# Attention followed by a two-layer block: P^T times V as plain float32 products, one head in each half of the array's columns

## Chip, cores and metric

The kernel runs on one core of a Trainium2 chip. The metric is device time in microseconds (us) for one execution, median over runs. The five engines that matter are TensorE (PE for its matmuls, PEld for its weight loads), VectorE (DVE), ScalarE (ACT), GpSimd (POOL) and SyncE (SP), whose queue issues the DMAs. Each engine works through its own queue in order; semaphores join them.

## Reference

Causal attention over 4 batches of 12 heads, 448 positions, head size 64, then a block with a leaky rectifier over 1792 tokens (768 to 2048 to 768), all in float32:

```
scores = scale * q @ k^T;  scores[above the diagonal] = -1e9
p = exp(scores - max(scores));  p = p / (sum(p) + 1e-9)
x = concat_heads(p @ v)                      # 1792 x 768
h = x @ w_in;  g = max(h, 0) + alpha * min(h, 0)
out = g @ w_out
```

The weights arrive as eight-byte floats and are decoded on the core.

## The kernel before, in words

**Attention.** Heads are worked on in 24 pairs (head 0 and head 1 of a pair, `j` in the code). A row of 448 positions is cut into 4 blocks of `CP` = 112. For a pair the steps are: `LQ`, `LK`, `LV` (loads, SP's queue); `S0` to `S2` (scores, L219: float32 matmuls with 64 rows, head 0 in the upper 64 rows of the array, head 1 in the lower 64); `MXij` (mask, and minimum of the negated scores, DVE, L232); `EXij` (exponential and row sum, ACT, L244); `RC` (reciprocal of the sums, two small DVE instructions, L252 and L253); `NOij` (scaling of a row block, POOL, L195); `PTi` (transposes of row block i through TensorE, L271); copies of the transposed blocks from PSUM into SBUF; `AV0` and `AV1` (the products with V, L313, one per head, both into one PSUM bank, transposed: 128 rows are the 2 x 64 columns of the two heads); `XH` (ACT, L191) and `XL` (DVE, L327), which split the result into a high part in float32r and a rest in float32r, as the matmuls of the second half want them. i is the row block, j the head.

**Products with V before.** For key blocks 0 and 1 (`c` < `NSP` = 2) P^T and V are each split in two float32r parts, and three float32r products are made: high by high, low by high, high by low. The split of P^T is `HIi` (ACT) and `LOi` (DVE, L288, PSUM minus the high part); that of V is `VH` (POOL, L195) and `VL` (POOL, L208). For key blocks 2 and 3 P^T is copied as it is (`FCi`, ACT) and the product is float32, which TensorE runs as two instructions for each matmul. V lies in SBUF with zeros beside it, so that each head's weights are 128 columns wide, of which 64 are zeros: both heads' products then add into the same 128 rows. `open_v` writes those zeros once at the start (three DVE fills, two DVE copies).

**Order.** `ORDER` is a list of steps written out by hand. In iteration n of the loop each entry is issued for pair n minus its lag (the number behind the plus); the letter behind the lag names the engine where there is a choice (a ACT, d DVE, p POOL). Four pairs are in flight: `S` has lag 1, most `MX` and `EX` lag 2, `PT` lag 3, `AV` lag 4. Every engine's queue follows this order. `ED` puts one instruction of the early decoding of the first weights (DVE, POOL or ACT) into each iteration from pair 4. PSUM has 8 banks, all from one pool; an iteration takes 13 of them, so that a product waits until another pair's result was read out.

**After attention.** Hooks (`after(...)`) place the first matmuls of the second half (`h_unit`, L381), their read-outs (`h_out`) and the decoding of further weights among the steps of the last two pairs. Then `h` (L381) and `o` (L415) matmuls alternate to the end.

Of the kernel before, what the change touches and what calls it, by code (L numbers as in the profile page):

```python
# [10 lines left out]
F32 = mybir.dt.float32  # L11
F32R = mybir.dt.float32r
# [4 lines left out]
ALU = mybir.AluOpType  # L17
# [4 lines left out]
CP = 112  # L22
# [2 lines left out]
FIRST = 3  # L25
LOADAT = 4, 12
ORDER = """
NO11+3p AV0+4 LK+1 MX11+2 EX10+2 EX20+2 AV1+4 MX00+2 EX11+2 EX00+2 PT0+3 PT1+3 LV+2 MX21+2 PT2+3 EX21+2 MX31+2 NO31+3p MX30+2 MX01+2 EX31+2 EX01+2 XH+4a NO30+3p PT3+3 HI0+3a XL+4 HI1+3a HI2+3a VL+3p LO0+3 LO1+3 S0+1 S1+1 ED+1 EX30+2 LO2+3 VH+2p FC2+3a LQ+0 RC+2 MX10+1 NO10+2p S2+1 NO21+2p NO01+2p HI3+3a LO3+3 NO00+2p NO20+2p MX20+1 FC3+3a
"""


# [1 line left out]
def kernel(  # L33
# [14 lines left out]
    nc = tc.nc  # L48
    B, NPAIR, D, _, S = qt.shape
# [1 line left out]
    DFF = w_out.shape[0]  # L51
    P = 128
    NCH = S // CP
    NSP = 2
    VB = 3
    KD = DM // P
    NH = DM // 2
    GC = 2
# [13 lines left out]
    def bank(name):  # L72
        return psa.tile([P, 512], F32, tag="a", name=name)

    ident = const.tile([P, P], F32, name="ident")
# [59 lines left out]


    att_a, att_b, ap = ExitStack(), ExitStack(), {}
    vz, vs = [], []

    def open_pools(stack, side, names):  # L140
        for name, bufs in names.items():
            ap[name] = stack.enter_context(
                tc.tile_pool(name="att_" + name, bufs=bufs, side=side, reuse_waits="tile")
            )

    def open_v():


        for n in range(VB):
            vz.append(ap["v"].tile([CP, NCH, 4 * D], F32, name=f"v{n}"))  # L150
            nc.vector.memset(vz[n].rearrange("p c (j u d) -> p (c j) u d", j=2, d=D)[:, :, 1], 0.0)
        for n in range(2):
            vs.append(ap["v"].tile([CP, NSP, 2, 3 * D], F32R, name=f"vs{n}"))
            nc.vector.tensor_copy(
                vs[n][:, :, :, D : 2 * D],
                vz[0][:, :NSP, D : 2 * D].unsqueeze(2).to_broadcast([CP, NSP, 2, D]),
            )

    def warm(n):

        ps = bank("warm")
        for _ in range(n):
            nc.tensor.matmul(ps, warm_sb[:, :P], warm_sb, start=True, stop=True)  # L163

    T = {}

    def half(j):
        return slice(j * D, (j + 1) * D)
# [12 lines left out]

    def load_v(p):
        b, hp = pairs[p]
        nc.sync.dma_start(
            out=vz[p % VB].rearrange("p c (j u d) -> p (c j) u d", j=2, d=D)[:, :, 0],
            in_=v[b, hp],
        )

    def copy(out, x, eng, side=1.0):
        if eng is nc.scalar:  # L190
            eng.activation(out, x, AF.Copy, scale=side)  # L191
        elif eng is nc.vector:
            eng.tensor_copy(out, x)
        else:
            eng.tensor_scalar(out=out, in0=x, scalar1=side, scalar2=1.0, op0=ALU.mult, op1=ALU.mult)  # L195

    def v_parts(p):
        t = vz[p % VB][:, :NSP].rearrange("p c (j u d) -> p c j u d", j=2, d=D)[:, :, :, 0]
        to = vs[p % 2].rearrange("p c u (a d) -> p c u a d", d=D)[:, :, :, ::2]
        return t, to[:, :, 0], to[:, :, 1]  # L200

    def v_hi(p, eng):
        t, hi, _ = v_parts(p)
        copy(hi, t, eng)

    def v_lo(p, eng):
        t, hi, lo = v_parts(p)
        eng.tensor_tensor(out=lo, in0=t, in1=hi, op=ALU.subtract)  # L208


    def scores(p, n):
# [46 lines left out]
        copy(t, t, eng, T["r", p][:, 2 * i + j : 2 * i + j + 1])  # L258


    def transpose_p(p, i):
        t = T["p", p, i]
        ps = {}
        for c0, c1 in ((0, min(i + 1, NSP)), (NSP, i + 1)):
            if c0 < c1:
                t0 = bank(f"pt_{p}_{i}_{c0}")[:CP, : 2 * (c1 - c0) * CP]
                t0 = T["pt", p, i, c0] = t0.rearrange("p (j c n) -> p j c n", j=2, n=CP)
                ps |= {c: t0[:, :, c - c0] for c in range(c0, c1)}
        for j in range(2):
            for c in range(i + 1):  # L270
                nc.tensor.transpose(ps[c][:, j], t[:, j, c * CP : (c + 1) * CP], ident[:CP, :CP])  # L271

    def pt_to(p, i, nm):

        t = T[nm, p]
        if i == 0:
            return t[:, :, :CP].rearrange("p j (c n) -> p j c n", n=CP)
        t = t[:, :, CP:].rearrange("p j (c r n) -> p j c r n", c=NSP, n=CP)
        return t[:, :, :, i - 1]

    def p_hi(p, i, eng):
        if ("pth", p) not in T:
            for nm in ("pth", "ptl"):
                T[nm, p] = ap["pt"].tile([CP, 2, S + S - CP], F32R, tag=nm, name=f"{nm}_{p}")
        copy(pt_to(p, i, "pth"), T["pt", p, i, 0], eng)

    def p_lo(p, i):
        nc.vector.tensor_tensor(  # L288
            out=pt_to(p, i, "ptl"), in0=T.pop(("pt", p, i, 0)), in1=pt_to(p, i, "pth"),
            op=ALU.subtract,  # L290
        )

    def p_full(p, i, eng):
        if ("ptf", p) not in T:
            T["ptf", p] = ap["pt"].tile([CP, 2, 3 * CP], F32, tag="ptf", name=f"ptf_{p}")
        o = T["ptf", p][:, :, :CP] if i == NSP else T["ptf", p][:, :, CP:]
        copy(o.rearrange("p j (c n) -> p j c n", n=CP), T.pop(("pt", p, i, NSP)), eng)

    def av(p, j):

        if j == 0:
            T["a", p] = bank(f"a_{p}")[:, :S]
        ps = T["a", p]
        for c in range(NCH):
            if c < NSP:
                h, l = [vs[p % 2][:, c, u, j * D : (j + 2) * D] for u in range(2)]
                ph, pl = [T[nm, p][:, j, c * S : (c + 1) * S - c * CP] for nm in ("pth", "ptl")]
                parts = (h, ph), (h, pl), (l, ph)
            else:
                w = vz[p % VB][:, c, j * D : (j + 2) * D]  # L310
                parts = [(w, T["ptf", p][:, j, : 2 * CP] if c == NSP else T["ptf", p][:, j, 2 * CP :])]
            for n, (w, x) in enumerate(parts):
                nc.tensor.matmul(  # L313
                    ps[:, c * CP :], w, x, start=(j == 0 and c == 0 and n == 0),
                    stop=(j == 1 and c == NCH - 1),
                )

    def x_cut(p):
# [7 lines left out]
        h, l = x_cut(p)  # L326
        nc.vector.tensor_tensor(out=l, in0=T.pop(("a", p)), in1=h, op=ALU.subtract)  # L327

    steps = {"LV": load_v, "RC": row_rec, "XL": x_lo}

    choice = {"VH": v_hi, "VL": v_lo, "XH": x_hi}

    def add(to, name, fn, *args):
        to[name] = lambda p, *eng: fn(p, *args, *eng)
# [3 lines left out]
    for n in range(NCH - 1):  # L338
        add(steps, f"S{n}", scores, n)
    for i in range(NCH):  # L340
        add(steps, f"PT{i}", transpose_p, i)
        add(choice, f"HI{i}", p_hi, i)
        add(steps, f"LO{i}", p_lo, i)
        if i >= NSP:
            add(choice, f"FC{i}", p_full, i)
        for j in range(2):
            add(steps, f"MX{i}{j}", row_max, i, j)
            add(steps, f"EX{i}{j}", row_exp, i, j)
            add(choice, f"NO{i}{j}", row_norm, i, j)
    for j in range(2):  # L350
        add(steps, f"AV{j}", av, j)
    steps["ED"] = lambda p: FIRSTED <= p and next(early, 0)

    order = []
    for w in ORDER.split():
        name, lag = w.split("+")
        if name in choice:
            eng = {"a": nc.scalar, "d": nc.vector, "p": nc.gpsimd}[lag[-1]]
# [99 lines left out]
    def early_chunk():  # L458

        before = iter(())  # L460
        for f in range(GC):
            for z in range(2):
                t = decode_piece("i", f, z)
                for _ in range(6):
                    next(t)
                    yield next(before, 0)
                before = t
        yield from before
# [15 lines left out]
    def after(p, name, fn, *args):  # L484
        hooks.setdefault((p, name), []).append(lambda: fn(*args))

    with tc.manual_schedule():
# [12 lines left out]
            out=mk, in_=mk, pattern=[[-1, CP]], compare_op=ALU.is_ge, fill=NEG, base=0,  # L500
            channel_multiplier=1,
        )
        nc.scalar.activation(maskb[:, S - CP :], mk, AF.Copy)
        warm(WARM)
        open_pools(att_b, "left", {"v": 1, "pt": 2, "b2": 2, "b4": 8, "p": 2})
        open_v()
        early = early_chunk()
        last = len(pairs) - 1

# [8 lines left out]
            after(last, name, early_steps)  # L518
        after(last, "S2", scores_done)
        after(last - 1, "PT3", h_next)  # L520
        after(last - 1, "FC3", h_finish)
        after(last - 1, "FC3", decode_start, 2)
        after(last - 1, "AV1", h_next)
        after(last, "PT3", h_next)
        after(last, "LO2", h_finish)
        after(last, "FC3", decode_finish, 2)
        after(last, "FC3", decode_start, 3)
        after(last, "AV1", h_next)
        after(last, "XH", h_finish)
        after(last, "XL", decode_finish, 3)  # L530
        after(last, "XL", h_finish)
# [63 lines left out]
```

## Time and profile before

| | us |
|---|---|
| median of 3 runs | 670.45 (668.53 to 670.71) |
| the profiled execution | 668.71 |
| its span, first to last instruction | 666.9 |
| PE busy (matmul) | 657.9 |
| DVE busy | 497.3 |
| POOL busy | 322.9 |
| ACT busy | 245.7 |
| share of the 16 DMA engines' span, main queue | 23.5% |

The profiled execution is one run; its span leaves out 1.8 us around it. Busy times are unions of an engine's instructions. A matmul's busy time includes its passage through the array, so that the ends of neighbours overlap; what a matmul costs is read from one start to the next.

### The profile page before, as it was taken

To read this page: it belongs to the slowest core of one execution; us is meant where nothing else is said; L and a number is where in the kernel's file an instruction comes from. 1 tells how busy PE (TensorE), PEld (TensorE's weight loads), DVE (VectorE), ACT (ScalarE), POOL (GpSimd) and SP (SyncE) were. 2 spreads that over 40 slices of the span, in tenths; PEclk is the share of its full clock that TensorE was granted. 3 is DMA by queue.
4 is the path that set the end of the run, shared out by engine and by line. 5 is a ranking of instruction groups with operands and counts; after the bars stand their busy time and mean duration, and the time that the engine had idled before them with its cause. 6 is when DMAs were issued, how large, how long until landed. Compare 5 with 4: busy or idle time off the path is not lost.

```text
span 666.9 us, 11216 instructions
## 1 busy us (share of the span) xinstructions
PE 657.9 (99%) x3852; PEld 591.3 (89%) x3852; DVE 497.3 (75%) x1266; ACT 245.7 (37%) x710; POOL 322.9 (48%) x442
## 2 busy tenths in 40 slices
PE   7999999999999999999999999999999999999998
PEld 4888888888878998999999899999989999998997
DVE  6788878888887585888687777778777777875444
ACT  6888999988932334111111111111111111111000
POOL 4566775666764545543435443344543334454110
PEclk9999999999999999999999999999999999999999
DMA  5533353333404131102203100220320022000223
GB/s 151 129 87 85 100 143 90 92 84 90 145 1 137 53 96 52 43 15 83 94 1 96 61 35 18 79 95 1 95 64 31 21 76 94 1 1 0 95 95 142
DMA packets 51256, 47.91 MB, mean 72 GB/s; under 512 B 26752, under 2 KB 45440, under 8 KB 51200
## 3 DMA queue, kind: packets, MB, share of 16 engines
q1 hardware_dynamic: 51200, 47.21, 23.5%
q8 instruction: 30, 0.49, 0.3%
q14 instruction: 26, 0.21, 0.1%
HBM read 41.69 MB, written 5.51 MB: 71 GB/s over the span
## 4 chain that ended last, share of the span: by engine, by line
PE 86%; POOL 5%; issue 4%; DVE 3%; ACT 1%; POOLq 0%; DVEq 0%
PE o L415 32%; PE h L381 30%; PE a L313 11%; PE s L219 7%; PE pt L271 6%; POOL p L195 2%; POOL gl L401 1%; PE warm L163 1%; ACT p L244 1%; POOL wi L130 1%; POOL wo L130 1%; POOL y_i L126 0%; POOL y_o L126 0%; DVE x_i L117 0%; DVE g L391 0%
## 5 line engine op out<-in xcount | busy, mean ns | idle before, releaser
L415 PE MATMUL o<-wo,gh 128*128 128x384 f32 x896 | 229.2, 336 | 0.4 <-DVE g L395 0.4
L381 PE MATMUL h<-xh,wi 128*128 128x512 f32 (+1 forms) x768 | 218.3, 364 | 0.3 <-DVE xl L327 0.3
L401 POOL TENSOR_TENSOR gl<-g,gh 128x512 fp32r<-128x512 f32 (+1 forms) x64 | 74.0, 1156 | 255.2 <-ACT gh L400 237.9
L415 PEld LDWEIGHTS o<-wo,gh 128*128 128x128 f32 x896 | 162.4, 188 | 2.5 <-DVE g L395 0.7
L381 PEld LDWEIGHTS h<-xh,wi 128*128 128x128 f32 x768 | 138.6, 189 | 22.7 <-DVE xl L327 0.5
L415 PE MATMUL o<-wo,gl 128*128 128x384 f32 x448 | 150.7, 336 | 0.0
L400 ACT ACTIVATE gh<-g 128x512 fp32r<-128x512 f32 (+1 forms) x64 | 37.0, 579 | 296.2 <-DVE g L395 296.2
L381 PE MATMUL h<-xl,wi 128*128 128x512 f32 (+1 forms) x384 | 139.4, 363 | 0.0
L423 DVE TENSOR_TENSOR acc<-o,acc 128x384 f32<-128x384 f32 x196 | 102.8, 552 | 42.6 <-PE o L415 41.8
L195 POOL TENSOR_SCALAR p<-p,rs 112x224 f32<-112x224 f32 (+1 forms) x192 | 92.9, 506 | 57.0 <-DVE rs L253 37.8
L244 ACT ACTIVATE p<-s,nm 112x224 f32<-112x224 f32 (+1 forms) x192 | 93.6, 498 | 22.9 <-DVE nm L232 22.9
L391 DVE TENSOR_SCALAR g<-h,alpha_sb 128x512 f32<-128x512 f32 (+1 forms) x64 | 43.4, 679 | 74.2 <-POOL gl L401 50.6
L415 PEld LDWEIGHTS o<-wo,gl 128*128 128x128 f32 x448 | 84.1, 188 | 0.0
L232 DVE CUSTOM_DVE_ANT_0 s<-s,maskb 112x224 f32<-112x224 f32 (+1 forms) x192 | 79.7, 476 | 4.6 <-PE s L219 4.6
L381 PEld LDWEIGHTS h<-xl,wi 128*128 128x128 f32 x384 | 72.4, 189 | 10.4
L313 PE MATMUL a<-pth,vs 112*128 112x448 f32 x192 | 61.5, 363 | 0.0
L271 PE MATMUL pt<-ident,p 112*112 112x112 f32 x480 | 51.6, 263 | 3.7 <-POOL p L195 2.6
L219 PE MATMUL s<-kr,qr 64*112 64x224 f32 (+3 forms) x384 | 55.2, 414 | 0.0
L288 DVE TENSOR_TENSOR ptl<-pt,pth 112x224 fp32r<-112x224 f32 (+1 forms) x96 | 51.4, 557 | 3.1 <-ACT pth L191 3.1
L271 PEld LDWEIGHTS pt<-ident,p 112*112 112x112 f32 x480 | 48.1, 136 | 5.2 <-POOL p L195 3.8
L313 PEld LDWEIGHTS a<-pth,vs 112*128 112x128 f32 x192 | 36.1, 188 | 15.9 <-ACT ptf L191 12.0
L191 ACT ACTIVATE pth<-pt 112x224 fp32r<-112x224 f32 (+1 forms) x96 | 43.3, 509 | 3.9 <-PE pt L271 3.9
(51 smaller groups left out, 720.0 us busy)
## 6 DMA issues: line engine op xcount, KB each, us to landing
wi<-in_moe_w_in_dram SPq DMA_DIRECT2D x32, 384.0 KB, 4.5
wo<-in_moe_w_out_dram SPq DMA_DIRECT2D x32, 384.0 KB, 5.6
qr<-in_q_dram SPq DMA_DIRECT2D x48, 112.0 KB, 2.7
kr<-in_k_dram SPq DMA_DIRECT2D x48, 112.0 KB, 2.7
v<-in_v_dram SPq DMA_DIRECT2D x24, 224.0 KB, 3.2
out_dram<-acc SPq DMA_DIRECT2D x13, 384.0 KB, 2.3
out_dram<-acc SPq DMA_DIRECT2D x2, 192.0 KB, 1.9
alpha_sb<-in_moe_alpha_dram SPq DMA_DIRECT2D x1, 8.0 KB, 5.6
```

Source lines behind the costliest of these rows:

```text
L195: eng.tensor_scalar(out=out, in0=x, scalar1=side, scalar2=1.0, op0=ALU.mult, op1=ALU.mult)
L219: nc.tensor.matmul(ps[:, o : o + lim], T["q", p][half(j), i * CP : (i + 1) * CP], T["k", p][half(j), :lim], start=(o == 0), stop=(n > 0 or ...
L232: nc.vector.tensor_tensor_reduce(out=t, in0=t, in1=maskb[:, (NCH - 1 - i) * CP :], scale=-SCALE, scalar=MOST_F32, op0=ALU.add, op1=ALU.min ...
L244: nc.scalar.activation(T["p", p, i][:, j], T.pop(("s", p, i, j)), AF.Exp, scale=-1.0, bias=T.pop(("nm", p, i, j)), accum_out=T["sm", p][:, ...
L271: nc.tensor.transpose(ps[c][:, j], t[:, j, c * CP : (c + 1) * CP], ident[:CP, :CP])
L288: nc.vector.tensor_tensor(out=pt_to(p, i, "ptl"), in0=T.pop(("pt", p, i, 0)), in1=pt_to(p, i, "pth"), op=ALU.subtract,)
L313: nc.tensor.matmul(ps[:, c * CP :], w, x, start=(j == 0 and c == 0 and n == 0), stop=(j == 1 and c == NCH - 1),)
L381: nc.tensor.matmul(ps[:, :T], w[kk], x[:, kk, t0 : t0 + T], start=(n == 0), stop=(n == 3 * KD - 1),)
L391: nc.vector.tensor_scalar(out=t[:, :T], in0=ps, scalar1=0.0, scalar2=alpha_sb[:, ch : ch + 1], op0=ALU.min, op1=ALU.mult,)
L401: nc.gpsimd.tensor_tensor(out=gl[:, :T], in0=t[:, :T], in1=gh[:, :T], op=ALU.subtract)
L415: nc.tensor.matmul(ps[:, :NH], x[:, t * P : (t + 1) * P], w, start=(n == 0), stop=(n == 3 * GC - 1),)
L423: nc.vector.tensor_tensor(out=a[:, cols], in0=ps[:, :NH], in1=a[:, cols], op=ALU.add)
```

## The change

P^T is copied out of PSUM as float32 for all four key blocks, and all products with V are float32: no high and low parts of P^T or V remain, and no zeros beside V. Head 0's product goes to PSUM rows 0 to 63 and head 1's to rows 64 to 127, each with weights of 64 columns, that is, through the first or the last 64 columns of the array. Row blocks 2 and 3 take one PSUM bank per head, and head 1's copies of them go to DVE (`C21`, `C31`), the rest to ACT (`C00` and `C10` both heads, `C20` and `C30` head 0). `ORDER` is new: `AV` is one step, `HI`, `LO`, `FC`, `VH`, `VL` are gone, `LV` has lag 3. V's pool holds three tiles. The hooks that hung on `FC3`, `LO2` and `AV1` hang on `C31`, `C21` and `AV`.

```diff
-NO11+3p AV0+4 LK+1 MX11+2 EX10+2 EX20+2 AV1+4 MX00+2 EX11+2 EX00+2 PT0+3 PT1+3 LV+2 MX21+2 PT2+3 EX21+2 MX31+2 NO31+3p MX30+2 MX01+2 EX31+2 EX01+2 XH+4a NO30+3p PT3+3 HI0+3a XL+4 HI1+3a HI2+3a VL+3p LO0+3 LO1+3 S0+1 S1+1 ED+1 EX30+2 LO2+3 VH+2p FC2+3a LQ+0 RC+2 MX10+1 NO10+2p S2+1 NO21+2p NO01+2p HI3+3a LO3+3 NO00+2p NO20+2p MX20+1 FC3+3a
+NO11+3p LK+1 MX11+2 EX10+2 EX20+2 AV+4 MX00+2 EX11+2 EX00+2 PT0+3 PT1+3 LV+3 MX21+2 PT2+3 EX21+2 MX31+2 NO31+3p MX30+2 MX01+2 EX31+2 EX01+2 XH+4a NO30+3p PT3+3 C00+3a XL+4 C10+3a C20+3a S0+1 S1+1 ED+1 EX30+2 C21+3d LQ+0 RC+2 MX10+1 NO10+2p S2+1 NO21+2p NO01+2p C30+3a NO00+2p NO20+2p MX20+1 C31+3d
...
+        T["v", p] = ap["v"].tile([CP, NCH, 2, D], F32, tag="v", name=f"v_{p}")
+        nc.sync.dma_start(out=T["v", p].rearrange("p c j d -> p (c j) d"), in_=v[b, hp])
...
+    def transpose_p(p, i, *heads):
         t = T["p", p, i]
+        for js in heads:
+            ps = bank(f"pt_{p}_{i}_{js[0]}")[:CP, : len(js) * (i + 1) * CP]
+            ps = T["pt", p, i, js] = ps.rearrange("p (j c n) -> p j c n", j=len(js), n=CP)
+            for j in js:
+                for c in range(i + 1):
+                    nc.tensor.transpose(
+                        ps[:, j - js[0], c], t[:, j, c * CP : (c + 1) * CP], ident[:CP, :CP]
+                    )
+
+    def pt_copy(p, i, js, eng):
         if ("ptf", p) not in T:
+            T["ptf", p] = ap["pt"].tile([CP, 2, 3 * NCH + 1, CP], F32, tag="ptf", name=f"ptf_{p}")
+        copy(T["ptf", p][:, js[0] : js[-1] + 1, i : 4 * i + 1 : 3], T.pop(("pt", p, i, js)), eng)
+
+    def av(p):
+        out = T["a", p] = bank(f"a_{p}")[:, :S]
         for c in range(NCH):
+            for j in range(2):
+                x = T["ptf", p][:, j].rearrange("p x n -> p (x n)")
                 nc.tensor.matmul(
+                    out[half(j), c * CP :], T["v", p][:, c, j],
+                    x[:, 4 * c * CP : (3 * c + NCH) * CP], start=(c == 0), stop=(c == NCH - 1),
                 )
...
+        heads = ((0, 1),) if i < 2 else ((0,), (1,))
+        add(steps, f"PT{i}", transpose_p, i, *heads)
+        for js in heads:
+            add(choice, f"C{i}{js[0]}", pt_copy, i, js)
...
-        open_pools(att_b, "left", {"v": 1, "pt": 2, "b2": 2, "b4": 8, "p": 2})
-        open_v()
+        open_pools(att_b, "left", {"v": 3, "pt": 2, "b2": 2, "b4": 8, "p": 2})
```

## Rows read from the trace of the kernel before

**Rows 1.** Busy time by stretch; columns: stretch, length, engines' busy us (instructions), clock, DMA.

```profile
0.00:19.84 19.84, 16.02 (x80) 8.80 (x81) 12.19 (x49) 12.34 (x42) 9.01 (x27) 0.91 0.48 128
19.84:180.34 160.50, 160.42 (x1178) 137.17 (x1177) 132.64 (x504) 143.91 (x486) 106.05 (x212) 1.00 0.41 109
180.34:220.90 40.56, 39.17 (x209) 33.88 (x209) 31.16 (x63) 14.84 (x38) 25.86 (x33) 1.00 0.23 79
```

**Rows 2.** The chain that ended last, in order of time: start us, us, piece.

```profile
19.91 3.51 PE a L313 x20
...
107.11 1.92 PE pt L271 x20
109.03 2.08 PE s L219 x16
...
172.55 3.54 PE a L313 x20
```

**Rows 3.** Groups by line and shape: count, busy us, mean ns of one, idle before.

```profile
L313 PE MATMUL a<-pth,vs 112*128 112x448 f32 x96 | 39.4, 410 | 0.0
...
L219 PE MATMUL s<-kr,qr 64*112 64x448 f32 x96 | 24.5, 545 | 0.0
```

**Rows 4.** Timeline of TensorE in one product with V: start us, us, instruction.

```profile
96.11 0.37 PE L313 MATMUL a<-ptl,vs 112*128 112x448 f32 x1
96.11 0.39 PEld L313 LDWEIGHTS a<-pth,vs 112*128 112x128 f32 x2
96.31 0.52 PE L313 MATMUL a<-pth,vs 112*128 112x448 f32 x2
...
96.97 0.75 PE L313 MATMUL a<-ptf,v 112*128 112x224 f32 x4
...
97.49 0.45 PE L313 MATMUL a<-pth,vs 112*128 112x448 f32 x1
```

**Rows 5.** Timeline of DVE over one period.

```profile
111.52 0.43 DVE L232 CUSTOM_DVE_ANT_0 s<-s,maskb 112x224 f32<-112x224 f32 x1
...
113.73 0.32 DVE L232 CUSTOM_DVE_ANT_0 s<-s,maskb 112x112 f32<-112x112 f32 x1
...
117.62 0.15 DVE L252 TENSOR_TENSOR sm<-sm,least 112x8 f32<-112x8 f32 x1
...
118.28 0.62 DVE L288 TENSOR_TENSOR ptl<-pt,pth 112x448 fp32r<-112x448 f32 x1
118.82 0.50 DVE L232 CUSTOM_DVE_ANT_0 s<-s,maskb 112x336 f32<-112x336 f32 x1
...
119.24 0.43 DVE L232 CUSTOM_DVE_ANT_0 s<-s,maskb 112x224 f32<-112x224 f32 x1
```

**Rows 6.** Timeline of ACT over the same period.

```profile
114.14 0.35 ACT L244 ACTIVATE p<-s,nm 112x112 f32<-112x112 f32 x1
114.39 0.19 ACT L244 ACTIVATION_READ_ACCUMULATOR p<-s,nm 112x1 f32 x1
114.67 0.55 ACT L191 ACTIVATE xh<-a 128x448 fp32r<-128x448 f32 x1
115.11 1.22 ACT L191 ACTIVATE pth<-pt 112x224 fp32r<-112x224 f32 x3
116.19 0.66 ACT L244 ACTIVATE p<-s,nm 112x448 f32<-112x448 f32 x1
116.71 0.23 ACT L244 ACTIVATION_READ_ACCUMULATOR p<-s,nm 112x1 f32 x1
116.80 0.39 ACT L191 ACTIVATE ptf<-pt 112x224 f32<-112x224 f32 x1
```

**Rows 7.** Timeline of POOL over the same period, with its idle time and who ended it.

```profile
114.30 0.73 POOL L208 TENSOR_TENSOR vs<-v,vs 112x256 fp32r<-112x256 f32 x1
...
118.24 0.97 POOL L195 TENSOR_SCALAR p<-p,rs 112x224 f32<-112x224 f32 x2 [2.84 <-DVE rs L253]
```

**Rows 8.** DMA issues of V: count, KB each, median us from issue to landing.

```profile
v<-in_v_dram SPq DMA_DIRECT2D x24, 224.0 KB, 3.2
```

More of the change, by code (lines that the diff above doesn't have):

```diff
@@ L53 @@
     NCH = S // CP
-    NSP = 2
-    VB = 3
     KD = DM // P
@@ L137 @@
     att_a, att_b, ap = ExitStack(), ExitStack(), {}
-    vz, vs = [], []
     def open_pools(stack, side, names):
@@ L143, in open_pools @@
                 tc.tile_pool(name="att_" + name, bufs=bufs, side=side, reuse_waits="tile")
[L144 to L156, printed above, removed]
             )
@@ L183, in load_v @@
         b, hp = pairs[p]
[L184 to L187, printed above, removed]
+        T["v", p] = ap["v"].tile([CP, NCH, 2, D], F32, tag="v", name=f"v_{p}")
+        nc.sync.dma_start(out=T["v", p].rearrange("p c j d -> p (c j) d"), in_=v[b, hp])
     def copy(out, x, eng, side=1.0):
@@ L195, in copy @@
             eng.tensor_scalar(out=out, in0=x, scalar1=side, scalar2=1.0, op0=ALU.mult, op1=ALU.mult)
[L197 to L208, printed above, removed]
     def scores(p, n):
@@ L258, in row_norm @@
         copy(t, t, eng, T["r", p][:, 2 * i + j : 2 * i + j + 1])
-    def transpose_p(p, i):
+    def transpose_p(p, i, *heads):
         t = T["p", p, i]
[L263 to L293, printed above, removed]
-        if ("ptf", p) not in T:
-            T["ptf", p] = ap["pt"].tile([CP, 2, 3 * CP], F32, tag="ptf", name=f"ptf_{p}")
-        o = T["ptf", p][:, :, :CP] if i == NSP else T["ptf", p][:, :, CP:]
-        copy(o.rearrange("p j (c n) -> p j c n", n=CP), T.pop(("pt", p, i, NSP)), eng)
@@ L299, in av @@
[L299 to L303, printed above, removed]
-        for c in range(NCH):
[L305 to L312, printed above, removed]
+        for js in heads:
[6 more added lines that the diff above has]
+                    )
@@ L313, in av @@
+    def pt_copy(p, i, js, eng):
+        if ("ptf", p) not in T:
+            T["ptf", p] = ap["pt"].tile([CP, 2, 3 * NCH + 1, CP], F32, tag="ptf", name=f"ptf_{p}")
+        copy(T["ptf", p][:, js[0] : js[-1] + 1, i : 4 * i + 1 : 3], T.pop(("pt", p, i, js)), eng)
+    def av(p):
+        out = T["a", p] = bank(f"a_{p}")[:, :S]
+        for c in range(NCH):
+            for j in range(2):
+                x = T["ptf", p][:, j].rearrange("p x n -> p (x n)")
                 nc.tensor.matmul(
-                    ps[:, c * CP :], w, x, start=(j == 0 and c == 0 and n == 0),
@@ L315, in av @@
-                    stop=(j == 1 and c == NCH - 1),
+                    out[half(j), c * CP :], T["v", p][:, c, j],
+                    x[:, 4 * c * CP : (3 * c + NCH) * CP], start=(c == 0), stop=(c == NCH - 1),
                 )
@@ L327, in x_lo @@
         nc.vector.tensor_tensor(out=l, in0=T.pop(("a", p)), in1=h, op=ALU.subtract)
-    steps = {"LV": load_v, "RC": row_rec, "XL": x_lo}
-    choice = {"VH": v_hi, "VL": v_lo, "XH": x_hi}
+    steps = {"LV": load_v, "RC": row_rec, "AV": av, "XL": x_lo}
+    choice = {"XH": x_hi}
     def add(to, name, fn, *args):
@@ L340 @@
     for i in range(NCH):
[L341 to L345, printed above, removed]
+        heads = ((0, 1),) if i < 2 else ((0,), (1,))
+        add(steps, f"PT{i}", transpose_p, i, *heads)
+        for js in heads:
+            add(choice, f"C{i}{js[0]}", pt_copy, i, js)
         for j in range(2):
@@ L349 @@
             add(choice, f"NO{i}{j}", row_norm, i, j)
-    for j in range(2):
-        add(steps, f"AV{j}", av, j)
     steps["ED"] = lambda p: FIRSTED <= p and next(early, 0)
@@ L520 @@
         after(last - 1, "PT3", h_next)
-        after(last - 1, "FC3", h_finish)
-        after(last - 1, "FC3", decode_start, 2)
-        after(last - 1, "AV1", h_next)
+        after(last - 1, "C31", h_finish)
+        after(last - 1, "C31", decode_start, 2)
+        after(last - 1, "AV", h_next)
         after(last, "PT3", h_next)
[L525 to L528, printed above, removed]
+        after(last, "C21", h_finish)
+        after(last, "C31", decode_finish, 2)
+        after(last, "C31", decode_start, 3)
+        after(last, "AV", h_next)
         after(last, "XH", h_finish)
```

## Prediction

> **What bounds the kernel now.** I read the busy times by stretch first. Attention in its steady state runs from 19.84 to 180.34 us, and there TensorE is busy for 160.42 of 160.50 us, while ACT has 143.9 (90%), DVE 132.6 (83%) and POOL 106.1 (66%) [rows 1]. The chain of waits says the same in order of time: it repeats three pieces on PE and nothing else, products with V (3.51), transposes (1.92), scores (2.08), 7.51 us together [rows 2]. From the first product on the chain (19.91) to one 20 periods later (172.55) a period is 7.63 us on average, so that 0.1 goes to small waits [rows 2]. The change shortens the first of the three pieces or lengthens it; what to look for next is how close the second busiest engines are. ACT's 90% is a warning.
>
> **PE, the products with V.** A float32r product of 448 columns goes from one start to the next in 0.20 us (96.11 to 96.31), 0.45 ns a column; the float32 ones, two instructions each of 224 and 112 columns, take 0.52 us for 672 columns (96.97 to 97.49), 0.77 ns a column in each of the two passes [rows 4]. Before, a pair has 2 x 3 x (448+336) float32r columns and 2 x 2 x (224+112) float32 ones, by these prices 2.1 and 1.0, with the restart for the second head about the 3.5 us of the chain. After, it has 2 x 2 x 1120 float32 columns, 3.45 us if the heads follow each other, half if they run side by side.
>
> No row shows two halves of the columns at once. The nearest is the scores: the same 1120 columns per head, the same two passes, the heads in two halves of the rows. 96 matmuls of 448 columns at 545 ns would be 52 us one by one; their busy time is 24.5, so two always run together. The products with V before do not: 96 x 410 ns is their whole 39.4 us [rows 3]. The scores of a pair, with a restart of the array on either side, take 2.08 us [rows 2]. I take 2.08 for the new products too, and keep 4.0 (each head's 1.89 after the other's, 0.2 for the restarts) as the other end. The transposes then follow a change of the array's shape, which I price at half of the 0.2, 0.1 us. PE's loop becomes 2.08 + 2.08 + 1.92 + 0.1 = 6.2 us.
>
> A rule of the Trainium skill speaks against this. The row first: while a matmul with 112 rows runs from 96.11 on, the weights of the next two, in the same rows, are already being loaded (0.39 us for both) and the next matmul starts 0.20 us later [rows 4]. The Trainium skill (TensorE: Matmul & The Clock Gate, Part 3, The mechanism) says that weight loads overlap running matmuls only where the row groups differ; by it the two heads, which share their rows, would pay for their loads. By that rule this is the third rival below; the row contradicts it, so it has a small chance.
>
> **The engines that PE waits for.** What is late next? I follow the new order around one period, on DVE and ACT, from the start of `C31` to the start of the next `C31`, with steps from one start to the next:
> - `C31`, 448 columns from PSUM on DVE: no row has this copy. `LO` reads the same 448 from PSUM and also SBUF: 0.54 (118.28 to 118.82) [rows 5]. A copy can't be expected to cost more; at best I allow 0.35. I take 0.54.
> - Six maxima: from `MX11` to the last, `MX01`, 2.21 (111.52 to 113.73) [rows 5].
> - `MX01` to `EX01` on ACT 0.41 (114.14), `EX01` 0.25 and 0.09 until ACT takes the next [rows 5, 6].
> - `XH` 0.44. It waited for PE before; now PE is ahead [rows 6].
> - `C00`, `C10`, `C20`: three copies of 224, 448 and 448 columns took 1.08; the third is now 336 wide, so 1.0 [rows 6].
> - `EX30` with its sum read out 0.75 (116.19 to 116.94) [rows 6].
> - `RC` and `MX10` 0.66 (117.62 to 118.28), `MX20` 0.42 (118.82 to 119.24) [rows 5].
>
> Sum 6.77 us, 6.8 with the hand-over to `RC`. It is a closed loop, for `C31` follows `MX20` on DVE and the next maxima follow `C31`. It is longer than PE's 6.2, so PE gets about 0.6 us of idle time per pair, before the products with V: head 1's first one needs `C31`. Before, the same loop had `LO3` in place of `C31` and a longer third copy, about 6.9, and hid behind PE's 7.5. What the change takes from ACT (two copies) and DVE (three of the four `LO`, against `C21`) lies outside this loop or in it only in part: off the path it frees engines, it doesn't shorten the period.
>
> With the 0.1 of small waits that today's periods have over their least (decoding instructions in ACT's and DVE's queues among them), I take 6.9. 21 periods between 19.84 and 180.34, each 7.63 - 6.9 = 0.73 shorter, give 15.4 us.
>
> **Edits with little price.** `VH` and `VL` leave POOL, which then waits longer for `RC`: it idles 2.84 us per period already [rows 7]. Their other effect is in the last pairs. There three products with V remain, each at most 1.3 shorter, but TensorE is busy for 39.17 of 40.56 us and DVE for 31.16, with the weights' decoding on the way [rows 1]; bounds 0 and 3.9, I take 2. `open_v`'s fills go from DVE's start: 12.19 of 19.84 us busy while PE is idle for 3.8, with the first scores awaited from PE [rows 1]; bounds 0 and 0.5, taken 0. `LV` is issued one iteration later and passes `LQ` and `LK` on SP's queue; with 3.2 us to landing it still arrives in the iteration before its product [rows 8], and it no longer waits for V's buffer, so nothing queues behind it; taken 0. PSUM: 13 banks per iteration before and after; `S2` now waits for `C20` and `C21` rather than for a `LO` and an `FC`, both done earlier in the loop; 0.
>
> **Sum.** 668.7 (the profiled execution, 1.7 below the median of the runs) - 15.4 - 2 = 651.3; forecast 651 us. With 0.2 either way per period and the bounds of the tail it lies between 643 and 658.
>
> **Rivals.**
> 1. *PE stays the bound.* If `C31` or the copies on ACT are cheaper, or PE's order covers the wait (head 0 runs on while head 1 waits), the period is 6.2 with 0.1 of small waits: 21 x 1.33 + 3.9 = 31.8, 637 us (634 to 643). For it: PE is the bound in every period now. Against: DVE's maxima alone are 2.21, and ACT waits for the last of them.
> 2. *The heads do not run side by side* (slower). Place: the products with V. 4.0 + 0.1 in place of 3.51 is 0.55 to 0.6 per pair, for 24 pairs some 13 us: 682 (677 to 690). It decides once the products take longer than 3.4 us. For it: no row shows halves of the columns, and both heads now read the same 112 partitions. Against: the scores.
> 3. *Weight loads stay exposed.* Eight loads per head of 0.19 or less (half the width, so taken at 0.14) add 1.1 to 2.08: 3.2 + 0.1, period 7.4, some 663 us; at the full 0.19, 673. Waits that lengthen the loop by 0.4 us end in the same place: 658 to 668.
>
> That the change does not do what it says cannot be: the products and copies are in the diff.
>
> **How the numbers follow.** Forecast 0.52, rival 1 0.16, rival 3 and longer loops 0.10, rival 2 0.19, and 0.03 for a result within 0.3% (2 us, about what a measurement of this kernel can tell). Faster 0.78, same 0.03, slower 0.19. The range 634 to 670 takes in the forecast, rivals 1 and 3 and the case of no change, 0.81 in all; rival 2 is left out.
>
> **What would show it.** In the profile after: scores and products with V of equal length (about 2.1 us, or a little more where head 1 starts late), with busy time about half of count times mean; a period of 6.9; DVE and ACT on the chain of waits in the steady stretch, where there was only PE; PE waiting for `C31` before head 1's first product. Products of 4 us would make it wrong at the root; a chain with PE alone and a period near 6.3 would make the loop wrong.

## The result, and the profile after

The changed kernel takes 651.59 us (median of 4 runs, 650.59 to 651.88) against 670.37 us: a ratio of 0.9723, 95% interval 0.9702 to 0.9743. The forecast was 651 us. The profiled execution took 651.64 us, with a span of 649.9 us.

Busy time by stretch, as in [rows 1]; the first three lines end at the first product with V, at the product of the last pair but two, and at the first `o` matmul; the last is a piece of the third.

```profile
0.00:19.46 19.46, 15.57 (x80) 9.15 (x81) 9.25 (x43) 11.63 (x41) 7.60 (x24) 0.91 0.43 118
19.46:163.69 144.23, 144.13 (x1094) 98.37 (x1092) 114.63 (x460) 127.15 (x443) 82.96 (x169) 1.00 0.44 122
163.69:203.38 39.69, 38.31 (x198) 28.83 (x197) 28.49 (x60) 13.69 (x36) 23.79 (x31) 0.96 0.24 81
...
170.53:176.45 5.92, 5.92 (x18) 4.44 (x18) 2.50 (x6) 2.29 (x6) 4.14 (x7) 0.71 0.00 0
```

The steady stretch holds the same 21 periods and is 160.50 - 144.23 = 16.3 us shorter; the start gives 0.4, and from 163.69 on there are 486.2 us in place of 486.6. That is the whole difference of the spans, 17.0 us. The two spans compare one execution with one: the profiled execution of the kernel before (668.71 us, mean granted clock 0.997) is 1.7 us under that kernel's median, and the medians differ by 18.8 us.

The chain of waits in order of time (start us, us, piece), one period, as in [rows 2]:

```profile
129.57 2.67 PE a L253 x14
132.23 2.06 PE pt L238 x20
134.29 2.08 PE s L188 x16
136.37 2.67 PE a L253 x14
```

A period is 6.80 us. The chain names PE alone, just as before, and PE is busy for 144.13 of 144.23 us. By these two views alone the new products with V would simply cost 2.67 us and PE would still be the bound. The groups by line and shape say that something is odd with them (count, busy us, mean ns of one):

```profile
L253 PE MATMUL a<-ptf,v 112*64 112x448 f32 x96 | 38.1, 565 | 0.1
...
L188 PE MATMUL s<-kr,qr 64*112 64x448 f32 x96 | 23.5, 541 | 0.0
```

If the 96 instructions ran one by one, they would be busy for 96 x 565 ns = 54.2 us; if two always ran together, for about half of that. Their busy time is 0.70 of it, where the scores' is 0.45. So the heads run together, but for part of the time one runs alone. The timeline of TensorE at the start of one product with V (from two narrow stretches) shows which:

```profile
136.30 0.59 PE L253 MATMUL a<-ptf,v 112*64 112x448 f32 x1
...
136.94 0.31 PEld L253 LDWEIGHTS a<-ptf,v 112*64 112x64 f32 x4 [0.44 <-DVE ptf L175]
```

Head 0 starts at 136.30; head 1's first weights are loaded at 136.94, 0.64 us later, released by DVE's copy `C31`. Those 0.6 us are not idle time of PE, since head 0's matmuls run on in their half of the columns.

DVE and ACT over the same period, to be read beside [rows 5] and [rows 6]. DVE, from one `C31` to the next:

```profile
129.46 0.62 DVE L175 COPY ptf<-pt 112x448 f32<-112x448 f32 x1
129.99 0.39 DVE L201 CUSTOM_DVE_ANT_0 s<-s,maskb 112x224 f32<-112x224 f32 x1
...
132.16 0.32 DVE L201 CUSTOM_DVE_ANT_0 s<-s,maskb 112x112 f32<-112x112 f32 x1
...
133.48 0.62 DVE L267 TENSOR_TENSOR xl<-a,xh 128x448 fp32r<-128x448 f32 x1 [0.94 <-ACT xh L173]
...
135.12 0.17 DVE L221 TENSOR_TENSOR sm<-sm,least 112x8 f32<-112x8 f32 x1
...
135.80 0.55 DVE L201 CUSTOM_DVE_ANT_0 s<-s,maskb 112x336 f32<-112x336 f32 x1
...
136.26 0.62 DVE L175 COPY ptf<-pt 112x448 f32<-112x448 f32 x1
```

ACT, `EX11` and then from `EX01` on:

```profile
130.54 0.45 ACT L213 ACTIVATE p<-s,nm 112x224 f32<-112x224 f32 x1 [0.23 <-DVE nm L201]
...
132.57 0.35 ACT L213 ACTIVATE p<-s,nm 112x112 f32<-112x112 f32 x1
...
132.92 0.53 ACT L173 ACTIVATE xh<-a 128x448 fp32r<-128x448 f32 x1
133.34 1.13 ACT L173 ACTIVATE ptf<-pt 112x224 f32<-112x224 f32 x3
134.33 0.66 ACT L213 ACTIVATE p<-s,nm 112x448 f32<-112x448 f32 x1
134.84 0.24 ACT L213 ACTIVATION_READ_ACCUMULATOR p<-s,nm 112x1 f32 x1
...
136.06 0.45 ACT L213 ACTIVATE p<-s,nm 112x224 f32<-112x224 f32 x1 [0.54 <-DVE nm L201]
```

Followed from `C31` to `C31`, there is no gap that PE would have to fill: `C31` 0.53, maxima 2.17, `MX01` to `EX01` 0.41, `EX01` 0.35, `XH` 0.42, three copies 0.99, `EX30` with its sum 0.75, hand-over 0.04, `RC` and `MX10` 0.68, `MX20` 0.46. The sum is 6.80 us, the period. `XH` no longer waits for PE. Beside the maxima ACT works through four exponentials without a pause, from `EX11` at 130.54 to 132.55, and DVE's last minimum is read out only 0.02 us before that: the two ways to `EX01` are equally long, so quicker maxima alone would hardly shorten this loop (no run tests it). The two idle times marked in brackets, DVE's 0.94 ahead of `XL` and ACT's 0.54 ahead of `EX10`, lie beside this path: each waits for the other engine.

### The profile page after: what moved, and what is told of

It is laid out like the page before. It is cut to its first block, busy times and chain, and to the rows that moved or that the text cites. A ratio compares the mean times of both kernels' runs of the same rounds, so it can differ in the third digit from the quotient of the medians.

```text
span 649.9 us, 10892 instructions
## 1 busy us (share of the span) xinstructions
PE 640.3 (99%) x3756; PEld 547.7 (84%) x3756; DVE 473.8 (73%) x1213; ACT 227.0 (35%) x662; POOL 296.6 (46%) x394
## 4 chain that ended last, share of the span: by engine, by line
PE 86%; POOL 5%; issue 4%; DVE 3%; ACT 1%; POOLq 0%; DVEq 0%
PE o L352 33%; PE h L318 31%; PE a L253 8%; PE s L188 7%; PE pt L238 7%; POOL p L177 2%; POOL gl L338 1%; ACT p L213 1%; PE warm L147 1%; POOL wi L128 1%; DVE s L201 1%; POOL wo L128 1%; POOL y_i L124 0%; POOL y_o L124 0%; DVE g L328 0%
## 5 line engine op out<-in xcount | busy, mean ns | idle before, releaser
L318 PEld LDWEIGHTS h<-xl,wi 128*128 128x128 f32 x384 | 72.9, 190 | 10.6
L253 PEld LDWEIGHTS a<-ptf,v 112*64 112x64 f32 x384 | 36.4, 136 | 39.3 <-issue 13.8
L253 PE MATMUL a<-ptf,v 112*64 112x448 f32 (+3 forms) x384 | 65.3, 406 | 0.1
L238 PE MATMUL pt<-ident,p 112*112 112x112 f32 x480 | 53.2, 266 | 4.0 <-POOL p L177 3.0
L188 PE MATMUL s<-kr,qr 64*112 64x224 f32 (+3 forms) x384 | 53.5, 410 | 0.0
L173 ACT ACTIVATE ptf<-pt 112x224 f32<-112x224 f32 (+1 forms) x96 | 41.0, 488 | 4.0 <-PE pt L238 4.0
L332 DVE SCALAR_TENSOR_TENSOR g<-h,g 128x512 f32<-128x512 f32 (+1 forms) x64 | 40.0, 625 | 2.2
```

The source lines that it names most:

```text
L188: nc.tensor.matmul(ps[:, o : o + lim], T["q", p][half(j), i * CP : (i + 1) * CP], T["k", p][half(j), :lim], start=(o == 0), stop=(n > 0 or ...
L238: nc.tensor.transpose(ps[:, j - js[0], c], t[:, j, c * CP : (c + 1) * CP], ident[:CP, :CP])
L253: nc.tensor.matmul(out[half(j), c * CP :], T["v", p][:, c, j], x[:, 4 * c * CP : (3 * c + NCH) * CP], start=(c == 0), stop=(c == NCH - 1),)
L318: nc.tensor.matmul(ps[:, :T], w[kk], x[:, kk, t0 : t0 + T], start=(n == 0), stop=(n == 3 * KD - 1),)
```

## Experiments

Four theories stand in the expectations. **L**: the closed loop over DVE and ACT sets the period, and PE waits for `C31` inside the product. **P**: PE is the bound, and the products take 2.67 us of themselves. **A**: the total work of ACT is the bound. **C** concerns the last pairs: TensorE's clock took back what was gained there. Every run is the changed kernel with one edit, but for the two that say so. The runs of the kernel before beside them had medians of 670.13 us (first four) and 670.53 us (last four).

### `C31` on ACT

```diff
-... MX20+1 C31+3d
+... MX20+1 C31+3a
```

> C31, head 1's copy of the last row block, goes from DVE to ACT, behind C30. Theory L (a closed loop over DVE and ACT sets the period of 6.81 us, TensorE waits 0.63 for C31): the loop loses C31's 0.54, the period falls to about 6.3, the products with V to about 2.1 us, some 641 us (638 to 645). Theory P (TensorE is the bound, the products take 2.67 of themselves because the two heads disturb each other): nothing moves, 651 us, products at 2.67. A third way: ACT, with 0.42 more per period, becomes the bound at 6.5 or more, 645 us or more.

Measured: 641.69 us (640.58 to 641.81), ratio to the kernel before 0.9576 (0.9559 to 0.9592), 10 us less than the changed kernel. The chain of waits of one period:

```profile
98.42 2.23 PE pt L238 x20
100.64 2.08 PE s L188 x16
102.72 2.04 PE a L253 x16
```

The products fall to 2.04 us and the period to 6.34. Theory P falls: nothing on TensorE was edited, and its products became 0.6 us shorter. ACT can carry the copy. What is late next stands in the transposes, 2.23 in place of 2.06; the list of who waited for whom in the steady stretch (us in total, times, longest) names POOL's scaling, 0.2 us in each of 19 periods:

```profile
PEld pt L238 <- POOL p L177: 3.8, 19, 0.4
```

### `C31` on ACT and `C00` on DVE

```diff
-... EX01+2 XH+4a NO30+3p PT3+3 C00+3a XL+4 ... MX20+1 C31+3d
+... EX01+2 C00+3d XH+4a NO30+3p PT3+3 XL+4 ... MX20+1 C31+3a
```

> As the run before, and C00 goes from ACT to DVE, ahead of XL, where DVE idles 0.9 us. Theory L: the loop is then 0.54 + 0.24 shorter, about 6.0, under TensorE's 2.04 + 2.06 + 2.08 = 6.18, so that TensorE is the bound again: period 6.2, products 2.04, some 639 us (636 to 643). Theory P: 651 us.

Measured: 637.07 us (636.01 to 638.17), ratio 0.951 (0.9488 to 0.9533). The timeline of TensorE over one period:

```profile
56.66 2.11 PE L253 MATMUL a<-ptf,v 112*64 112x448 f32 x16
58.70 2.13 PE L238 MATMUL pt<-ident,p 112*112 112x112 f32 x20
60.76 2.15 PE L188 MATMUL s<-kr,qr 64*112 64x224 f32 x16
62.84 0.60 PE L253 MATMUL a<-ptf,v 112*64 112x448 f32 x2
```

From one start to the next 2.04, 2.06 and 2.08, a period of 6.18 us with nothing waiting: PE is the bound again, though only just. In the steady stretch ACT (the fourth busy time) is busy for 127.80 of 130.36 us:

```profile
19.60:149.96 130.36, 130.24 (x1094) 87.58 (x1092) 113.22 (x460) 127.80 (x443) 83.20 (x169) 1.00 0.47 135
```

The group of the 448-column products shows the heads side by side all the time, 23.3 us busy of 96 x 565 ns = 54.2:

```profile
L253 PE MATMUL a<-ptf,v 112*64 112x448 f32 x96 | 23.3, 565 | 0.0
```

This version is 14.5 us faster than the changed kernel, from two edits to the list of steps, one instruction each.

### Full width: float32, but no column halves

```diff
-                    out[half(j), c * CP :], T["v", p][:, c, j],
-                    x[:, 4 * c * CP : (3 * c + NCH) * CP], start=(c == 0), stop=(c == NCH - 1),
+                    out[:, c * CP :], vz[p % 3][:, c, j * D : (j + 2) * D],
+                    x[:, 4 * c * CP : (3 * c + NCH) * CP], start=(c == 0 and j == 0),
+                    stop=(c == NCH - 1 and j == 1),
```

V is loaded between zeros, as in the kernel before.

> Undoes the column halves alone: float32 and all copies as after the change, but V with zeros beside it and weights of 128 columns, both heads adding into the same 128 rows. Both theories: the two heads follow each other, products 3.45 to 3.6 us, period about 7.6, some 671 us (667 to 675), as much as before the change. If the gain came from the fewer copies on ACT and DVE rather than from the halves, it stays near 652.

Measured: 677.49 us (676.08 to 678.49), ratio 1.0112 (1.0087 to 1.0136): 1.1% slower than the kernel before. The timeline of TensorE over one period:

```profile
96.84 2.08 PE L247 MATMUL pt<-ident,p 112*112 112x112 f32 x20
98.85 2.15 PE L197 MATMUL s<-kr,qr 64*112 64x224 f32 x16
100.93 4.09 PE L262 MATMUL a<-ptf,v 112*128 112x448 f32 x16
104.86 0.64 PE L247 MATMUL pt<-ident,p 112*112 112x112 f32 x5
```

From start to start the products take 3.92 to 3.93 us, and the 21 periods average 8.01. The column halves alone are worth 677.5 - 651.6 = 25.9 us (24.1 of them in the steady stretch; 1.3 arose in the start-up of this profile); float32 throughout, without them, costs 7.4 us against the split products. The freed engines (the fewer copies on ACT and DVE) shortened nothing here: transposes, scores and products follow each other on PE without a gap. My expectation was 6 us too low: I had 0.77 ns for a column of a float32 pass, from a stretch whose last matmul was followed early [rows 4]. With 0.19 us off for the restart, (3.92 - 0.19) us / 4480 columns is 0.83 ns.

### Head by head

```diff
-        for c in range(NCH):
-            for j in range(2):
+        for j in range(2):
+            for c in range(NCH):
```

> The same products in the same halves, but issued all of head 0 first, then all of head 1 (c inside j). If TensorE runs the halves side by side only when they alternate in its queue: products about 3.9, period 8.05, some 679 us. If it takes head 1's instructions ahead of head 0's waiting ones from further back: products 2.1 to 2.7, 652 us. Theories L and P say the same here; it asks what the halves need.

Measured: 667.79 us (one run), neither of the two values expected. The timeline of TensorE over one product (from several narrow stretches):

```profile
112.55 3.47 PE L253 MATMUL a<-ptf,v 112*64 112x448 f32 x16
...
113.93 0.59 PE L253 MATMUL a<-ptf,v 112*64 112x448 f32 x2
...
115.96 2.13 PE L238 MATMUL pt<-ident,p 112*112 112x112 f32 x20
```

The products take 3.41 us, 0.51 less than one after the other at full width. In the trace head 1's first matmul (448 columns) starts at 113.93 together with head 0's fifth, when three of head 0's eight are still to come. It did not wait for its data: `C31` had ended at 112.95. TensorE thus took a matmul for the free half past three that waited for the other half, but no further. The full gain came only with the heads alternating in the queue.

### A spare copy on ACT, inside and outside the loop

```diff
+    def spare(p):
+        t = ap["b2"].tile([CP, S], F32, tag="spare", name=f"spare_{p}")
+        nc.scalar.activation(t, maskb, AF.Copy)
...
-... EX01+2 XH+4a
+... EX01+2 XX+3 XH+4a
```

> The changed kernel with one spare copy of 448 columns per iteration on ACT, between EX01 and XH, that is, inside the loop (its result is not used). Theory L: the period grows by the whole copy, 0.42 to 0.45, to about 7.25, some 661 us. Theory P, or a loop that does not pass through XH: nothing moves, 652 us.

Measured: 662.15 us (one run), 10.6 us more. The period is 7.27, longer by 0.46; the copy takes 0.47 from its start to the start of `XH`:

```profile
97.53 2.50 PE s L188 x14
100.03 2.71 PE a L253 x13
102.74 2.06 PE pt L238 x20
```

In the second run the same copy stands behind `C30` (`C30+3a XX+3`).

> The same spare copy behind C30, where ACT idles 0.5 to 0.7 us per period while it waits for MX10. Theory L: period 6.8, 652 us. If ACT's total work were the bound (theory A), 661 us as in the run before.

Measured: 652.67 us (one run). The steady period is unchanged, 6.80:

```profile
97.31 2.67 PE a L253 x14
99.97 2.06 PE pt L238 x20
102.03 2.08 PE s L188 x16
```

The same instruction on the same engine costs its whole length in one place and nothing in the other. Theory A falls, and the loop runs through `XH`, as theory L has it. (The 1.1 us of the second run against the changed kernel's median are not the copy's. Its first product with V came at 21.74 us rather than 19.46, after a longer stretch at half clock in the start-up, and its last pairs were 1.6 us shorter, for the clock did not fall there; the part on the tail below comes back to it.)

### The second half's first matmuls earlier

```diff
-        after(last - 1, "PT3", h_next)
+        after(last - 1, "PT1", h_next)
```

> The changed kernel with the first matmuls of the second half (18 of h) issued before PT2 of the last pair but one, not after its PT3, so that TensorE has work while POOL is late with the scaling there. Theory C (the tail gave nothing back because TensorE idled 1.3 us in those transposes and then ran 3.4 us at half clock): h takes 4.25 instead of 5.92, no stretch at half clock after 100 us, 649 to 650 us. If the wait only moves to the next product with V, or the clock falls all the same: 651 to 652 us.

Measured: 650.33 us (649.99 to 651.97); in the profiled execution, 649.99 us, the 18 matmuls took 4.22 us, and the granted clock was 1.00 from 166.66 to 176.07 us:

```profile
166.66:176.07 9.41, 8.46 (x55) 7.02 (x55) 7.19 (x18) 4.50 (x13) 5.29 (x9) 1.00 0.00 0
```

As theory C expects, but the ranges of the runs overlap with the changed kernel's (650.59 to 651.88). In this one profile the stretch at half clock is gone; that the median moved is not shown. Among executions with the same mean granted clock there is little between the two kernels: at 0.997 this one took 649.99, 650.13 and 650.53 us, the changed kernel 650.59; at 0.995 they took 651.97 and 651.88. Part of the wait only moved: TensorE now idles 0.95 us ahead of the next product.

The fastest version with the same edit:

> The fastest version so far (C31 on ACT, C00 on DVE) with the same 18 matmuls issued earlier. It had no half-clock stretch (h 4.28), so only TensorE's idle time of 1.8 us in those transposes is to be had: 635 to 637 us.

Measured: 637.11 us (635.76 to 638.38), no different from the 637.07 without it. Its profiled execution lost 2 us in the start-up, where the clock was at half for 6.8 us rather than 3.4, so the small gain that was looked for can't be seen in it. Nor do the executions at a mean granted clock of 0.997 show one: 635.76 and 636.48 us here, 636.01 and 636.02 without the edit.

## Why the prediction was right

**PE's terms.** The scores were the right row for the products: undisturbed, the products take 2.04 us (forecast 2.08). The transposes take 2.06 from one start to the next, against 2.01 in the kernel before:

```profile
99.23 2.08 PE L271 MATMUL pt<-ident,p 112*112 112x112 f32 x20
101.24 0.45 PE L219 MATMUL s<-kr,qr 64*112 64x224 f32 x2
```

So they became 0.05 longer behind the new products. The forecast had 1.92 + 0.1, with the 1.92 of the chain, whose pieces begin a little later than the instructions; the total, 2.02, was near. PE's loop is 6.18 us (forecast 6.2), as the run with `C31` on ACT and `C00` on DVE shows by itself.

**The loop over DVE and ACT.** Forecast 6.77 by its steps, 6.8 with the hand-over; measured 6.80, with no step off by more than 0.04 (`C31` 0.53 for 0.54, the maxima 2.17 for 2.21, `MX20` 0.46 for 0.42). That it is this loop that sets the period was only argued then; the spare copy in two places and the two moves of `C31` and `C00` show it now. That the copies which the change takes from DVE and ACT outside the loop are worth nothing was not run by itself; the spare copy behind `C30`, which cost nothing, speaks for it. One detail was off: PE's 0.6 us of waiting stand inside the products, on head 1's side, and not ahead of them.

**The allowance.** I took 6.9 with 0.1 of small waits; the average of the 21 periods is 144.23 / 21 = 6.87. Forecast for the stretch 15.4 us, measured 16.3.

**The tail**, the term that was mis-sized: 2 us forecast, 0.3 measured. The two last products did become 1.2 to 1.3 us shorter each, and the one before them 0.5. But TensorE's clock fell. The transposes behind the product of the last pair but two, and the 18 matmuls of `h` that follow, as in [rows 1], in the kernel before:

```profile
183.78:187.46 3.68, 2.29 (x23) 1.86 (x21) 2.67 (x7) 1.59 (x6) 1.58 (x2) 1.00 0.00 0
187.46:191.71 4.25, 4.25 (x18) 3.48 (x19) 3.18 (x7) 2.65 (x7) 2.67 (x4) 1.00 0.01 2
```

In the changed kernel, with the piece at the lower clock:

```profile
166.59:170.53 3.94, 2.56 (x22) 1.91 (x21) 2.93 (x8) 1.56 (x7) 1.67 (x2) 1.00 0.00 0
...
171.16:174.57 3.41, 3.41 (x10) 2.64 (x9) 1.87 (x5) 1.66 (x5) 2.50 (x4) 0.50 0.00 0
```

The `h` matmuls from 170.53 on take 5.92 us at a mean granted clock of 0.71, against 4.25 at 1.00; 3.41 us of them are at 0.50, the lower level of 1.2 GHz. That is 1.7 us, the size of what is missing. The run with the spare copy behind `C30` shows the same stretches without the fall:

```profile
168.86:172.79 3.93, 2.56 (x21) 1.91 (x20) 2.92 (x8) 1.55 (x7) 1.67 (x2) 1.00 0.00 0
172.79:177.10 4.31, 4.31 (x19) 3.30 (x19) 2.51 (x6) 2.76 (x7) 2.76 (x4) 1.00 0.00 0
```

There, with the spare copies still on ACT, everything from the product of the last pair but two (165.96) to the end of the span (650.9) takes 484.9 us, 1.6 less than in the kernel before. So for a tail at full clock the forecast of 2 was nearly right; that the clock could fall was not in the sum. The start gave 0.4 where I had put 0.

**Luck in the number.** The stretch gave 0.9 us more than forecast, the start 0.4 more, the tail 1.7 less; in the sum these nearly cancel, and 651.3 stands against 651.64. The sum also starts from one execution, 668.7; from the median of 670.37 it would have given 653.

**Rivals.** PE did not stay the bound: the runs say what it took to make it so, two instructions on other engines. The heads run side by side, so the slower case falls; its price (4.0 us, 682) was near, for one after the other at full width they take 3.92 us and the kernel 677.49. Weight loads: in that run with `C00` on DVE 16 matmuls with 64-column weights follow in 2.04 us although the heads share their rows; worked out as for the full-width run, at 0.83 ns a column and 0.19 us for the restart, the two passes of a head (2240 columns) alone come to 2.05. The rule of the Trainium skill that loads overlap only across row groups (TensorE: Matmul & The Clock Gate, Part 3, The mechanism) does not show here; the measurement decides.

**What the profile was to show**, also wrong in one point: I expected DVE and ACT on the chain of waits, and PE to show a wait. The chain names PE alone, for head 0's matmuls cover head 1's wait. And with `C31` on ACT and `C00` on DVE, where PE is the bound, the chain goes through ACT. There the two loops are nearly equal, and the chain shows only one of them.

## What to carry to other kernels

When PE becomes faster, add up the next loop before counting the gain: follow one engine's queue from an instruction to its next occurrence, across the engines it hands to, with start-to-start times; here a copy in that loop cost its full length, and the same copy in an engine's idle stretch nothing. A half-filled array reads as busy: compare busy time with count times mean before believing that TensorE is the bound. Two products with 64 weight columns each ran side by side in the halves of the array when they alternated in the queue.

## What the runs showed of the hardware that was not expected

- TensorE let a matmul for the free half of the columns overtake matmuls that waited for the other half, but only a few: in the head-by-head run it started with three of the other head's eight still waiting (products 3.41 us, between 2.04 alternating and 3.92 at full width).
- The granted clock fell to 0.50 for 3.41 us at 171.16 in the changed kernel's profile. PE had been busy for 2.56 of the 3.94 us before 170.53. In the kernel before, the same transposes had 2.29 busy of 3.68 us, and with the spare copy behind `C30` 2.56 of 3.93; in both the clock stayed at 1.00 in the `h` matmuls behind them. It fell at the same place in the profiles of the first run (`C31` on ACT; 4.51 us of transposes, `h` 5.91) and of the spare copy inside the loop (4.41 and 5.91), and not in that of the run with `C00` on DVE as well (3.85 and 4.28). What makes the difference between 3.94 and 3.93 stays open.
